# The experts' places in the gathered tensor, loaded as 448 rows each instead of by their own sizes

## The chip, the cores and the metric

One core of a Trainium2 chip. The metric is device time in microseconds of one execution, the median of three runs. The engines are TensorE (PE; its weight loads are listed as PEld), VectorE (DVE), ScalarE (ACT), GpSimd (POOL) and SyncE (SP). SP issues nearly all plain transfers, GpSimd the scattered ones.

## What is computed

Three stages on float32 data: a linear attention with decay, a mixture of 8 experts of which each token takes the best one, and a mixture of 4 experts of which each token takes all, weighted.

```
state = alpha[:, :, t, :, None] * state + k[:, :, t] (x) v[:, :, t];  y[:, :, t] = q[:, :, t] . state
x = y as (3072, 384)
logits = normed(x) @ normed(expert_emb).T / tau;  expert_idx = argmax(logits)
for e in range(8):                      # first mixture
    mask = expert_idx == e
    out[mask] = gate_w[mask, None] * (relu(x[mask] @ w1[e]) @ w2[e])
for e in range(4):                      # second mixture, x = out of the first
    out += p[:, e:e + 1] * (relu(x @ w1[e]) @ w2[e])
```

3072 tokens of 384 numbers; w1 is 384 x 1024 and w2 is 1024 x 384 for each expert.

## The kernel before

`attention_and_routing` computes the attention on all engines, chooses each token's expert and scatters the token's row (GpSimd, `scatter`) into the DRAM tensor `xs`, which has 3072 rows for each of the 8 experts. The first 448 rows of each expert were filled with zeros before (`prefill`). It also sorts the experts: place 0 is expert 0, places 1 to 7 are the others from the most chosen to the least. Where the text says "expert e" of the first mixture, it means the place e.

`experts` then runs the two mixtures. The list `WIN` (line 26) says how many tokens the fast path takes at each place: 448, 448, 432, 416, 404, 396, 392, 384; `W0` is the largest, 448. Place e goes through these steps:

- `window(e)` (lines 147 to 158) loads its rows from `xs` into a tile `xw` of 112 partitions, four rows (6144 bytes) to a partition. The transfer is issued by SP, line 154. For e above 0 the expert's number stands in a register of SP. The tile has two buffers.
- `xpose(e)` transposes the tile on PE (line 175) into PSUM; ScalarE copies it to `xh` (line 180), DVE puts the rest into `xl` (line 181), so that the product is made of three matmuls of reduced width.
- Eight units f follow, each with its own weights: `gemm1` (lines 120 to 122, 9 matmuls into `h`), `h_split` (ScalarE's `hh` in line 111, DVE's `hl` in line 112) and `g2` (lines 208 to 210, 9 matmuls from `hh` and `hl` into `o`). `g2` runs one unit behind `gemm1`.

The weights of one unit are 384 KB. `load_w` (line 57, SP) brings them into `wraw`, three buffers; `split_w` makes the two parts of `wu` from them, the first on ScalarE (line 67), the second on GpSimd (line 68), ten buffers. A new load waits until GpSimd has emptied a buffer. In unit (e, f) the program splits the unit nine places ahead, before it comes to the matmuls and to `h_split`.

Each engine takes its instructions in the order of the program. In unit f = 1 of place e it comes, for SP, to the weight load of that unit, then to `window(e + 2)`, then to the next weight loads. For ScalarE it comes to the split of a weight unit (line 67), then to `hh` of the current unit (line 111). In units 3 to 5 the three blocks of the next place are transposed.

The second mixture works on all 3072 tokens with the same units and loads nothing but weights.

Of the kernel before, what the change touches and what calls it, by code (L numbers as in the profile page):

```python
# [17 lines left out]
B, H, S, D = 4, 8, 768, 48  # L18
# [3 lines left out]
KD = DM // 128  # L22
NG = 8
CW = 129
# tokens that the fast path takes in: expert 0, then the others from the most chosen to the least
WIN = [448, 448, 432, 416, 404, 396, 392, 384]
W0 = max(WIN)
NR = 3072
# [3 lines left out]
@with_exitstack  # L32
def tile_main(ctx: ExitStack, tc: tile.TileContext, a: dict, out: bass.AP):
    nc = tc.nc

    const = ctx.enter_context(tc.tile_pool(name="const", bufs=1))
    small = ctx.enter_context(tc.tile_pool(name="small", bufs=2))
    dram = ctx.enter_context(tc.tile_pool(name="dram", bufs=1, space=bass.MemoryType.DRAM))

    xs = dram.tile([E1 * NR, DM], F32, name="xs")  # L40
    info_d = dram.tile([NT, 8], F32, name="info_d")

    # ---------------------------------------------------------------- weights
    units = [(0, e, f) for e in range(E1) for f in range(NFB)]
    units += [(1, e, f) for e in range(E2) for f in range(NFB)]
    wraw, wtile, ids = {}, {}, {}
    w_loaded, w_split = [0], [0]

    def load_w(n):
        while w_loaded[0] < min(n, len(units)):  # L50
            u = w_loaded[0]
            t = wst.tile([128, 2 * DM], F32, tag="wraw", name="wraw")
            src = a["wu"][u]
            if NFB <= u < E1 * NFB:
                e = a["wu"][0:E1 * NFB].rearrange("(e f) r c -> e f r c", f=NFB)
                src = e[bass.ds(ids[u // NFB], 1), u % NFB].rearrange("o r c -> (o r) c")
            nc.sync.dma_start(out=t, in_=src)
            wraw[u] = t
            w_loaded[0] += 1

    def split_w(n):
        while w_split[0] < min(n, len(units)):
            u = w_split[0]
            load_w(u + 1)
            r = wraw.pop(u)
            t = wun.tile([128, 2, 2 * DM], F32R, tag="wu", name="wu")
            nc.scalar.activation(out=t[:, 0], in_=r, func=AF.Copy)  # L67
            nc.gpsimd.tensor_tensor(out=t[:, 1], in0=r, in1=t[:, 0].bitcast(F32), op=ALU.subtract)  # L68
            wtile[u] = t
            w_split[0] += 1  # L70

    with tc.manual_schedule():
        ti = const.tile([128, 2, 128], F32, name="ti")
        ident = ti[:, 1]
        inf = const.tile([128, 24, 8], F32, name="inf")
        keep = {
            "ident": ident,
            "ti": ti,
            "ordi": const.tile([128, 8], I32, name="ordi"),
            "offi": const.tile([128, 8], I32, name="offi"),  # L80
            "posi": const.tile([128, 24], I32, name="posi"),
            "inf": inf,
            "flag": const.tile([1, 1], I32, name="flag"),
        }
        with ExitStack() as fast:
            wun = fast.enter_context(tc.tile_pool(name="wun", bufs=10))
            wst = fast.enter_context(tc.tile_pool(name="wst", bufs=3))
            scat = attention_and_routing(tc, a, small, keep, xs, info_d, wst, load_w, split_w)
            experts(fast, tc, a, keep, small, xs, info_d, scat, wtile, ids, load_w, split_w, out)

    bad = nc.values_load(keep["flag"][0:1, 0:1], min_val=0, max_val=1000)
    with tc.If(bad > 0):
        general(tc, a, ident, out)


def experts(ctx, tc, a, keep, small, xs, info_d, scat, wtile, ids, load_w, split_w, out):
# [24 lines left out]
            nc.tensor.matmul(ps, lhsT=w[:, 1, ks], rhs=xh(k), start=False, stop=False)  # L121
            nc.tensor.matmul(ps, lhsT=w[:, 0, ks], rhs=xl(k), start=False, stop=(k == KD - 1))  # L122

    # token info in the order of the experts
    infs = []

    def info(u):
# [11 lines left out]
    with ExitStack() as c1:  # L139
# [7 lines left out]
        def window(e):  # L147
            t = xwp.tile([W0 // 4, 4, DM], F32, tag="xw", name="xw")
            src = xs[0:W0, :]
            if e:  # L150
                src = xs.rearrange("(e r) d -> e r d", r=NR)[bass.ds(ids[e], 1), 0:WIN[e]].rearrange("o r d -> (o r) d")
            cs = [slice(k * 128, k * 128 + 128) for k in range(KD)] if e == 0 else [slice(0, DM)]
            for c in cs:
                ins = nc.sync.dma_start(
                    out=t[0:WIN[e] // 4, :, c], in_=src[:, c].rearrange("(p j) d -> p j d", j=4)
                )
                after(ins, scat, "all rows")
            xws[e] = t
# [146 lines left out]
def attention_and_routing(tc, a, small, keep, xs, info_d, wst, load_w, split_w):  # L305
# [5 lines left out]
    with ExitStack() as ctx:  # L311
# [18 lines left out]
        tau = c1.tile([128, 1], F32, name="tau")  # L330
# [6 lines left out]
        half = c1.tile([128, 6], F32, name="half")  # L337
# [29 lines left out]
        def c3(t, w):  # L367
            return t.rearrange("p (c w) -> p c w", w=w)

        # decay products of a chunk: after each step to its end (G), and their inverses (bf)  # L370
        def prep1(g, pp, c0=0, c1=3, part=2):
            al = tins[g, pp]
            lo, hi = 2 * CW * c0, 2 * CW * c1
# [178 lines left out]
        def route_b(r):  # L552
            u0, u1 = groups[r]
            n, sl = u1 - u0, slice(u0, u1)
            rt, mx, pr = state.pop(r)
            sv = small.tile([128, n, 8], F32, tag="sv", name="sv")
            si = small.tile([128, n], I32, tag="si", name="si", bufs=4)
            rank = [
                lambda: nc.vector.tensor_tensor(out=sv, in0=pr, in1=ohb[:, sl, :], op=ALU.mult),
                lambda: nc.vector.tensor_reduce(out=slotf[:, sl], in_=sv, op=ALU.add, axis=AX.X),  # L560
                lambda: nc.vector.tensor_scalar(
                    si, slotf[:, sl], float(E1 * NR - 1), 0.0, op0=ALU.min, op1=ALU.max
                ),
            ]
            g, root = root_v(nc, small, rt, ssq[:, sl], n, 128, "n")
            ex, exps = soft(nc, small, g, raw[:, sl, :], mx, n)
            # two chains of small steps, turn by turn
            chain = root + exps
            while rank or chain:
                for c in (rank, chain):  # L570
                    if c:
                        c.pop(0)()
            state[r] = si, ex
            if r < len(groups) - 1:
                count(r)
# [27 lines left out]
                tc.add_to_no_dep_group("xs", ins.ins)  # L603
                scat.append(ins)

        # ------------------------------------------------------------ start
        load_in(0, 0, 0, 259)
        nc.sync.dma_start(out=hmask, in_=a["hmask"])
        load_in(0, 0, 775, 1287)
# [166 lines left out]
        nc.vector.memset(ones, 1.0)  # L776
        nc.vector.memset(offc, 0.0)
        nc.vector.tensor_copy(cnt, pc)
        # the order of the experts: each one's number of experts before it, and each place's expert
        nc.vector.scalar_tensor_tensor(out=key, in0=cnt, scalar=8.0, in1=kadd, op0=ALU.mult, op1=ALU.add)  # L780
        nc.vector.tensor_tensor(out=gt3, in0=rows(key), in1=cols(key), op=ALU.is_gt)
        nc.vector.tensor_reduce(out=num, in_=gt3, op=ALU.add, axis=AX.X)
        nc.vector.tensor_tensor(out=sel, in0=rows(num), in1=cols(iot), op=ALU.is_equal)
        dot(srt, sel, iot)
        nc.vector.tensor_scalar(keep["ordi"], srt, float(E1 - 1), 0.0, op0=ALU.min, op1=ALU.max)
        # first columns of the places; as they are if no count is over its window, and else such that all is written
        dot(srt, sel, cnt)
        nc.vector.tensor_tensor(out=num, in0=srt, in1=wins, op=ALU.min)
        nc.vector.tensor_tensor_scan(offc[:, 1:8], ones[:, 1:8], num[:, 0:7], 0.0, op0=ALU.mult, op1=ALU.add)
        nc.vector.tensor_tensor(out=keep["offi"], in0=offc, in1=loff[:, 0, :], op=ALU.max)  # L790
        # places of the tokens in the order of the experts
        dot(off, gt3, cnt)
        nc.vector.tensor_tensor(out=off, in0=off, in1=loff[:, 1, :], op=ALU.subtract)
        pv = wk.tile([128, NU, 8], F32, tag="At", name="pv")
# [4 lines left out]
        nc.vector.tensor_reduce(out=pf, in_=pv, op=ALU.add, axis=AX.X)  # L799
        nc.vector.tensor_tensor(out=pf, in0=pf, in1=slotf, op=ALU.add)  # L800
        nc.vector.tensor_scalar(keep["posi"], pf, float(NT - 1), 0.0, op0=ALU.min, op1=ALU.max)
        # what the fast path doesn't cover
        fl = c1.tile([128, 3], F32, name="fl")
        ft = c1.tile([128, 3], F32, name="ft")
        nc.vector.memset(fl, 0.0)
# [17 lines left out]


def root_v(nc, pool, r, ss, n, parts, tag):
    """Twice the square root of ss from a first value r, to float32's accuracy: the tile and the steps."""
    g = pool.tile([parts, n], F32, tag=tag + "g", name="sq_g")
    return g, [
        lambda: nc.vector.tensor_scalar(g, r, 1e-18, None, op0=ALU.max),
# [10 lines left out]


def choose(nc, pool, wcon, raw, oh, n):
    """One-hot choice of the first largest of 8 (into oh), and the largest."""
    mx = pool.tile([128, n], F32, tag="mx", name="mx")
    nc.vector.tensor_reduce(out=mx, in_=raw, op=ALU.max, axis=AX.X)
    key = pool.tile([128, n, 8], F32, tag="key", name="key")
# [6 lines left out]


def soft(nc, pool, g2, raw, mx, n):
    """Exponentials of the logits less their largest, and the steps; g2 is twice the lengths of the rows."""
    rd = pool.tile([128, n], F32, tag="rd", name="rd")
    lg = pool.tile([128, n, 8], F32, tag="lg", name="lg")
    ex = pool.tile([128, n, 8], F32, tag="ex", name="ex")
# [15 lines left out]


def scale_rows(nc, pool, es_in, es, r, tau):
    """Rows of es_in over (their length + 1e-6) and tau, in place; es is their square sums."""
    g = run(root_v(nc, pool, r, es, 1, 8, "e"))
    nc.vector.tensor_scalar(g, g, 0.5, 1e-6, op0=ALU.mult, op1=ALU.add)  # L880
    nc.vector.tensor_scalar(g, g, tau[0:8, 0:1], None, op0=ALU.mult)
# [2 lines left out]


def general(tc, a, ident, out):
    """Any decay and any choice of experts: step by step over time, every expert over every token."""
    nc = tc.nc
    with ExitStack() as ctx:
        gc = ctx.enter_context(tc.tile_pool(name="gc", bufs=1))  # L890
# [153 lines left out]
def layout(inputs):  # L1044
# [2 lines left out]
    q, k, al = (np.asarray(inputs[n]) for n in ("q", "k", "alpha"))  # L1047

    def pairs(x):
        # -> (b, half, pp, row=(s d), chunk, pair in pp, 128)  # L1050
        x = x.reshape(B, 2, 2, 2, 2, 3, 128, D)  # b pp j s hf c i d
        return x.transpose(0, 4, 1, 3, 7, 5, 2, 6).reshape(NG, 2, 96, 3, 2, 128)

    aqk = np.zeros((NG, 2, 96, 775 + 1536), np.float32)
# [69 lines left out]
```

## Time and profile before

| | |
|---|---|
| median of 3 runs | 1264.83 us (1263.66 to 1265.12) |
| span of the profiled execution | 1262.2 us |
| its own time beside the span | not listed apart; the median is 2.6 us above the span |
| PE busy | 1192.4 us, 94% of the span |
| DVE, ACT, POOL busy | 426.1, 350.5, 320.9 us |
| mean granted TensorE clock | 0.972 |
| loads of `xw` | 10: three of 224.0 KB for place 0, and 672.0, 648.0, 624.0, 606.0, 594.0, 588.0, 576.0 KB for places 1 to 7 |

Times in rows are microseconds from the span's start. PE's matmuls are pipelined: a row's duration includes its filling, and the pace is read from the starts. A wait is put down to the instruction or the transfer that ended last before the waiting one began. "Granted clock" is the share of TensorE's full speed, 2.4 GHz.

### The profile page before, as it was taken

To read this page: it belongs to the slowest core of one execution; us is meant where nothing else is said; L and a number is where in the kernel's file an instruction comes from. 1 tells how busy PE (TensorE), PEld (TensorE's weight loads), DVE (VectorE), ACT (ScalarE), POOL (GpSimd) and SP (SyncE) were. 2 spreads that over 40 slices of the span, in tenths; PEclk is the share of its full clock that TensorE was granted. 3 is DMA by queue.
4 is the path that set the end of the run, shared out by engine and by line. 5 is a ranking of instruction groups with operands and counts; after the bars stand their busy time and mean duration, and the time that the engine had idled before them with its cause. 6 is when DMAs were issued, how large, how long until landed. Compare 5 with 4: busy or idle time off the path is not lost.

```text
span 1262.2 us, 16110 instructions
## 1 busy us (share of the span) xinstructions
PE 1192.4 (94%) x6565; PEld 1089.2 (86%) x6565; DVE 426.1 (34%) x791; ACT 350.5 (28%) x624; POOL 320.9 (25%) x223
## 2 busy tenths in 40 slices
PE   6987896987999999999999999999999999999996
PEld 4876785976999999999999999999999999999996
DVE  8998974221322222222222222212222222222221
ACT  3555553433544421111221111131111121111111
POOL 4565644544676620000130000040000021111111
PEclk9987897997999999999999999999999999999998
DMA  8845515423443420000020000020000010000000
GB/s 248 280 138 155 152 39 179 132 88 102 133 132 115 126 65 1 1 1 1 13 88 1 1 1 1 1 76 25 1 1 1 1 39 1 26 25 26 25 26 28
DMA packets 31260, 78.68 MB, mean 62 GB/s; under 512 B 7419, under 2 KB 12795, under 8 KB 29833
## 3 DMA queue, kind: packets, MB, share of 16 engines
q1 hardware_dynamic: 27337, 68.02, 17.7%
q0 software_dynamic: 3840, 9.54, 2.1%
q8 instruction: 53, 0.87, 0.3%
q14 instruction: 30, 0.25, 0.1%
HBM read 62.41 MB, written 15.14 MB: 61 GB/s over the span
## 4 chain that ended last, share of the span: by engine, by line
PE 81%; DVE 9%; DMA 4%; issue 3%; ACT 1%; POOL 1%; SPq 0%; ACTq 0%; POOLq 0%; DVEq 0%
PE h L120 13%; PE h L122 13%; PE h L121 13%; PE p L269 10%; PE p L268 10%; PE p L267 10%; PE o L208 3%; PE o L209 3%; PE o L210 3%; DMA wraw<-in_wu_dram 2%; DVE bf L393 2%; DVE G L380 2%; DVE At L443 1%; DMA v<-in_v_dram 1%; PE xt L175 1%
## 5 line engine op out<-in xcount | busy, mean ns | idle before, releaser
L112 DVE SCALAR_TENSOR_TENSOR hl<-h,hh 128x512 fp32r<-128x512 f32 (+8 forms) x264 | 171.9, 651 | 762.0 <-ACT hh L111 754.8
L68 POOL TENSOR_TENSOR wu<-wraw,wu 128x768 fp32r<-128x768 f32 x96 | 178.1, 1856 | 677.4 <-ACT wu L67 658.6
L111 ACT ACTIVATE hh<-h 128x512 fp32r<-128x512 f32 (+8 forms) x264 | 149.2, 565 | 670.4 <-PE h L122 668.7
L269 PE MATMUL p<-wu,hl 128*128 128x384 f32 x768 | 258.9, 337 | 0.0
L268 PE MATMUL p<-wu,hh 128*128 128x384 f32 x768 | 258.2, 336 | 0.0
L267 PE MATMUL p<-wu,hh 128*128 128x384 f32 x768 | 258.1, 336 | 0.0
L120 PE MATMUL h<-x,wu 128*128 128x512 f32 (+1 forms) x600 | 233.0, 388 | 0.0
L122 PE MATMUL h<-x,wu 128*128 128x512 f32 (+1 forms) x600 | 230.6, 384 | 0.0
L121 PE MATMUL h<-x,wu 128*128 128x512 f32 (+1 forms) x600 | 228.0, 380 | 0.0
L268 PEld LDWEIGHTS p<-wu,hh 128*128 128x128 f32 x768 | 144.3, 188 | 7.4
L267 PEld LDWEIGHTS p<-wu,hh 128*128 128x128 f32 x768 | 144.4, 188 | 7.1
L269 PEld LDWEIGHTS p<-wu,hl 128*128 128x128 f32 x768 | 144.3, 188 | 0.0
L122 PEld LDWEIGHTS h<-x,wu 128*128 128x128 f32 x600 | 112.6, 188 | 26.6
L121 PEld LDWEIGHTS h<-x,wu 128*128 128x128 f32 x600 | 112.8, 188 | 16.1
L120 PEld LDWEIGHTS h<-x,wu 128*128 128x128 f32 x600 | 112.8, 188 | 14.5
L67 ACT ACTIVATE wu<-wraw 128x768 fp32r<-128x768 f32 x96 | 80.8, 843 | 93.1 <-PE o L210 35.5
L208 PE MATMUL o<-hh,wu 128*128 128x448 f32 (+6 forms) x192 | 68.4, 356 | 14.5 <-ACT hh L111 14.5
L120 PE MATMUL h<-xh,wu 128*128 128x448 f32 (+6 forms) x192 | 70.4, 367 | 0.0
L280 POOL DMA_INDIRECT out_dram<-acc,toki x24 | 23.4, 974 | 183.4 <-DVE acc L276 178.5
L209 PE MATMUL o<-hl,wu 128*128 128x448 f32 (+6 forms) x192 | 68.4, 356 | 0.0
L438 PE MATMUL A<-qb,G 96*128 96x256 f32 x192 | 55.6, 435 | 13.6 <-ACT qb L415 8.3
L121 PE MATMUL h<-xh,wu 128*128 128x448 f32 (+6 forms) x192 | 68.4, 356 | 0.0
(150 smaller groups left out, 1172.9 us busy)
## 6 DMA issues: line engine op xcount, KB each, us to landing
wraw<-in_wu_dram SPq DMA_DIRECT2D x96, 384.0 KB, 3.0
tin<-in_aqk_dram SPq DMA_DIRECT2D x14, 866.6 KB
xs<-pre SPq DMA_DIRECT2D x8, 672.0 KB, 9.5
v<-in_v_dram SPq DMA_DIRECT2D x8, 576.0 KB, 5.3
tin<-in_aqk_dram SPq DMA_DIRECT2D x2, 384.0 KB, 6.8
xw<-xs SPq DMA_DIRECT2D x3, 224.0 KB
xw<-xs SPq DMA_DIRECT2D x1, 672.0 KB
xw<-xs SPq DMA_DIRECT2D x1, 648.0 KB
```

Of the source, the lines that this page charges most:

```text
L67: nc.scalar.activation(out=t[:, 0], in_=r, func=AF.Copy)
L68: nc.gpsimd.tensor_tensor(out=t[:, 1], in0=r, in1=t[:, 0].bitcast(F32), op=ALU.subtract)
L111: nc.scalar.activation(out=hh[:, 0:n], in_=ps, func=AF.Relu)
L112: nc.vector.scalar_tensor_tensor(out=hl[:, 0:n], in0=ps, scalar=0.0, in1=hh[:, 0:n].bitcast(F32), op0=ALU.max, op1=ALU.subtract)
L120: nc.tensor.matmul(ps, lhsT=w[:, 0, ks], rhs=xh(k), start=(k == 0), stop=False)
L121: nc.tensor.matmul(ps, lhsT=w[:, 1, ks], rhs=xh(k), start=False, stop=False)
L122: nc.tensor.matmul(ps, lhsT=w[:, 0, ks], rhs=xl(k), start=False, stop=(k == KD - 1))
L208: nc.tensor.matmul(o, lhsT=w[:, 0, ds], rhs=hh[:, 0:n], start=(f == 0), stop=False)
L209: nc.tensor.matmul(o, lhsT=w[:, 0, ds], rhs=hl[:, 0:n], start=False, stop=False)
L267: nc.tensor.matmul(o, lhsT=hh[:, js], rhs=w[:, 0, DM:2 * DM], start=(f == 0), stop=False)
L268: nc.tensor.matmul(o, lhsT=hh[:, js], rhs=w[:, 1, DM:2 * DM], start=False, stop=False)
L269: nc.tensor.matmul(o, lhsT=hl[:, js], rhs=w[:, 0, DM:2 * DM], start=False, stop=(f == NFB - 1))
```

## The change

The loads for places 1 to 7 take 448 rows of the expert, and the whole tile of 112 partitions, instead of `WIN[e]` rows and a quarter as many partitions. `xpose` still reads `WIN[e] // 4` partitions. Nothing else is changed; some comments are gone.

```
             src = xs[0:W0, :]
             if e:
-                src = xs.rearrange("(e r) d -> e r d", r=NR)[bass.ds(ids[e], 1), 0:WIN[e]].rearrange("o r d -> (o r) d")
+                src = xs.rearrange("(e r) d -> e r d", r=NR)[bass.ds(ids[e], 1), 0:W0].rearrange("o r d -> (o r) d")
             cs = [slice(k * 128, k * 128 + 128) for k in range(KD)] if e == 0 else [slice(0, DM)]
             for c in cs:
                 ins = nc.sync.dma_start(
-                    out=t[0:WIN[e] // 4, :, c], in_=src[:, c].rearrange("(p j) d -> p j d", j=4)
+                    out=t[:, :, c], in_=src[:, c].rearrange("(p j) d -> p j d", j=4)
                 )
```

The order of the instructions is the same on every engine. On SP's queue this is one of the six places that differ, the load for place 4 (line 154) between SP's register work (line 186) and the next weight load (line 57):

```order
 L186 ISA x2
 L154 ISA
-L154 DMA xw<-xs 101x1536
+L154 DMA xw<-xs 112x1536
 L57 ISA
 L57 DMA wraw<-in_wu_dram 128x768
```

No row moved; the transfer's shape went from 101 to 112 partitions of 1536 numbers. The places 2, 3, 5, 6 and 7 go from 108, 104, 99, 98 and 96 to 112 in the same way, and place 1 has 112 in both.

## Rows read from the trace of the kernel before

**Rows 1.** The page: span, and TensorE's busy time, share and instructions.

```profile
span 1262.2 us, 16110 instructions
...
PE 1192.4 (94%) x6565; PEld 1089.2 (86%) x6565; DVE 426.1 (34%) x791; ACT 350.5 (28%) x624; POOL 320.9 (25%) x223
```

**Rows 2.** Waits of PE, 203 to 1262 us: total, times, longest.

```profile
PE o L208 <- ACT hh L111: 14.5, 1, 14.5
```

**Rows 3.** By stretches: length, busy time (instructions) per engine, clock, DMA share, GB/s.

```profile
300.00:400.00 100.00, 100.00 (x557) 98.16 (x556) 29.12 (x51) 47.81 (x80) 66.33 (x43) 1.00 0.41 130
400.00:760.00 360.00, 360.00 (x1851) 330.66 (x1850) 85.30 (x138) 77.46 (x125) 50.04 (x29) 1.00 0.10 30
```

**Rows 4.** Timeline of PE: start, duration, line, operation, idle time before it.

```profile
276.82 0.36 PE L120 MATMUL h<-xh,wu 128*128 128x432 f32 x1
...
278.42 0.35 PE L122 MATMUL h<-xl,wu 128*128 128x432 f32 x1
293.26 0.73 PE L208 MATMUL o<-hh,wu 128*128 128x432 f32 x1 [14.49 <-ACT hh L111]
...
296.95 0.69 PE L175 MATMUL xt<-ti,xw 104*128 104x104 f32 x4
297.42 0.44 PE L120 MATMUL h<-xh,wu 128*128 128x432 f32 x1
...
301.38 0.44 PE L120 MATMUL h<-xh,wu 128*128 128x432 f32 x1
```

**Rows 5.** Timeline of ACT.

```profile
266.29 0.85 ACT L67 ACTIVATE wu<-wraw 128x768 fp32r<-128x768 f32 x1 [1.35 <-PE o L210]
...
270.31 0.84 ACT L67 ACTIVATE wu<-wraw 128x768 fp32r<-128x768 f32 x1
271.65 0.53 ACT L111 ACTIVATE hh<-h 128x432 fp32r<-128x432 f32 x1 [0.50 <-PE h L122]
291.95 0.84 ACT L67 ACTIVATE wu<-wraw 128x768 fp32r<-128x768 f32 x1 [19.77 <-DMA wraw<-in_wu_dram]
292.70 0.51 ACT L111 ACTIVATE hh<-h 128x432 fp32r<-128x432 f32 x1
```

**Rows 6.** The chain of work that ended last, in order of time: start, duration, what.

```profile
265.39 26.46 DMA wraw<-in_wu_dram
```

**Rows 7.** DMA issues: queue, operation, count, size, median time to landing.

```profile
wraw<-in_wu_dram SPq DMA_DIRECT2D x96, 384.0 KB, 3.0
...
xw<-xs SPq DMA_DIRECT2D x1, 606.0 KB
```

**Rows 8.** Timeline of SP's queue: start, duration, issue.

```profile
202.58 2.61 SPq L154 DMA_DIRECT2D xw<-xs  x2
...
263.38 0.29 SPq L154 DMA_DIRECT2D xw<-xs  x1
...
265.39 5.77 SPq L57 DMA_DIRECT2D wraw<-in_wu_dram  x1
```

**Rows 9.** Line 57 by itself: ns of one issue, min/median/max, first and last start.

```profile
L57 SPq DMA_DIRECT2D wraw<-in_wu_dram x96: 327/333/5772, 50.3 to 1034.4; - x96
```

**Rows 10.** By stretches, between the load for place 4 and PE's next matmul.

```profile
265.00:270.00 5.00, 5.00 (x26) 4.64 (x25) 1.98 (x4) 2.60 (x5) 3.20 (x3) 1.00 0.06 24
...
280.00:285.00 5.00, 0.00 (x0) 0.00 (x0) 0.00 (x0) 0.00 (x0) 0.00 (x0) 0.86 0.06 26
285.00:290.00 5.00, 0.00 (x0) 0.00 (x0) 0.00 (x0) 0.00 (x0) 0.00 (x0) 0.50 0.07 27
```

**Rows 11.** By stretches, at the loads of 104, 99, 98 and 96 partitions.

```profile
232.00:236.00 4.00, 4.00 (x21) 3.65 (x20) 0.63 (x1) 1.70 (x3) 1.85 (x1) 1.00 0.80 222
...
310.00:314.00 4.00, 4.00 (x22) 3.82 (x21) 0.61 (x1) 1.46 (x3) 3.08 (x3) 1.00 0.76 247
339.00:343.00 4.00, 4.00 (x23) 3.92 (x22) 0.59 (x1) 1.36 (x2) 3.26 (x3) 1.00 0.83 268
367.00:371.00 4.00, 4.00 (x24) 4.00 (x23) 0.58 (x1) 1.48 (x3) 3.28 (x3) 1.00 0.89 259
```

**Rows 12.** The DMA queues from 206 to 232 us, GB/s in 40 equal slices.

```profile
GB/s 271 180 255 345 317 241 222 227 189 147 57 24 0 255 321 28 38 189 345 85 274 251 123 232 255 24 0 24 246 326 9 0 0 25 184 340 66 14 0 0
```

**Rows 13.** Waits of ACT, 195 to 470 us.

```profile
ACT wu L67 <- DMA wraw<-in_wu_dram: 22.6, 4, 19.8
```

More of the change, by code (lines that the diff above doesn't have):

```diff
@@ L150, in window @@
             if e:
-                src = xs.rearrange("(e r) d -> e r d", r=NR)[bass.ds(ids[e], 1), 0:WIN[e]].rearrange("o r d -> (o r) d")
+                src = xs.rearrange("(e r) d -> e r d", r=NR)[bass.ds(ids[e], 1), 0:W0].rearrange("o r d -> (o r) d")
             cs = [slice(k * 128, k * 128 + 128) for k in range(KD)] if e == 0 else [slice(0, DM)]
@@ L154, in window @@
                 ins = nc.sync.dma_start(
-                    out=t[0:WIN[e] // 4, :, c], in_=src[:, c].rearrange("(p j) d -> p j d", j=4)
+                    out=t[:, :, c], in_=src[:, c].rearrange("(p j) d -> p j d", j=4)
                 )
```

## The prediction

> **What bounds the kernel now.** I read first where TensorE is idle, since it is busy for 1192.4 us of 1262.2 [rows 1]. The list of its waits from 203 us to the end has a single entry: 14.5 us, once, in L208 for ScalarE's hh [rows 2]. The table by stretches agrees: PE is busy 100.00 of 100 and 360.00 of 360 us after it, at full clock [rows 3]. So behind 203 us this kernel is TensorE work end to end with one hole, and a change to the loads of the expert part can gain only in that hole, or lose by making new ones.
>
> Second, what the hole is. PE's last matmul before it starts at 278.42, the next one at 293.26 [rows 4]. ScalarE's order of work tells why: after the hh of 271.65 it should split the next weight unit (L67), and that waits 19.77 us for a load of wraw. The hh that PE wants (292.70) stands behind it on the same engine [rows 5]. That up to ten split units lie ready doesn't help, because it is ScalarE's queue that is blocked, not the supply of split weights.
>
> Third, which load that is. The chain of waits runs through a wraw load issued at 265.39, which takes 26.46 us [rows 6], where such a load takes 3.0 in the median of 96 [rows 7]. On SP's queue the instruction ahead of it is the load of expert 4's place (263.38), and SP needs 5.77 us to issue the weight load behind it [rows 8], against a median of 0.333 [rows 9]. While nothing but this is in flight, the DMA engines are busy by 0.06 to 0.07 of the sixteen and move 24 to 27 GB/s [rows 10]: that is one engine out of sixteen. Expert 4's load is 404 rows, 101 partitions, 101 x 6144 B = 620,544 B (606.0 KB in [rows 7]); at 25 GB/s this is 24.8 us. From about 264.4 us it would end near 289, and the part of the weight loads that lies behind it on that engine accounts for the rest up to 291.85. The sum closes: one engine carries the whole 101-partition load, the weight load waits for its turn there, ScalarE for the weight load, PE for ScalarE.
>
> The other loads of this line do nothing of the kind. Those of 104, 99, 98 and 96 partitions stand in stretches with 0.76 to 0.89 of all engines busy at 222 to 268 GB/s, and PE is busy 4.00 of 4 us in each [rows 11].
>
> **Why one engine.** The rows show that 101 partitions went through one engine and that 104, 99, 98 and 96 went through many; they do not show the rule. The nearest row to the new load is expert 1's, which has today the very form that all get: 112 partitions, 672 KB, a source chosen by a register. It was issued from 202.58 on, together with the next one [rows 8], and at 213.8 us (the thirteenth of 40 slices of 0.65 us from 206 on) nothing is moved at all [rows 12]; on one engine at 25 GB/s its 688,128 B would need 27.5 us, to 230. So the form with 112 is wide. The Trainium skill, "DMA: Bandwidth & Descriptors", section "Why a DMA increments its semaphore by 16 and not by 1", has the rule: a DMA uses the largest count up to 16 that divides the slowest dimensions, by which 108, 104, 101, 99, 98 and 96 partitions get 12, 13, 1, 11, 14 and 16 engines and 112 gets 16. The trace agrees for 101 (0.06 of sixteen) and doesn't separate the others; by that rule the sum below is the same as by the rows.
>
> **The change, part by part.**
> 1. *The 101-partition load becomes a 112-partition one.* It removes the hole. Its cost is read between like points on PE. L120 of one unit starts at 276.82; the next unit begins, after 18 matmuls and 4 transposes, at 297.42. The same step takes 301.38 - 297.42 = 3.96 us one unit later at full clock [rows 4]. So the unit should have started at 280.78, and 297.42 - 280.78 = **16.64 us** is lost. Of these, 293.26 - 278.62 = 14.64 are the hole (278.42 plus one matmul step; eight steps from 276.82 on take 1.60, so one is 0.20), and 2.0 the clock: in the hole the granted clock fell from 1.00 to 0.50, that is from 2.4 to 1.2 GHz [rows 3, 10], and the nine matmuls after it take 296.95 - 293.26 = 3.69 us for 1.80 [rows 4]. Nothing of this lies beside other work of PE, and all of PE's later work follows directly, so all of it comes off the end.
> 2. *What comes in its place at that point.* 688,128 B over many engines. At the 222 to 268 GB/s of [rows 11] that is 2.6 to 3.1 us, and with the 393,216 B of the weight load behind it 4.0 to 4.9 us after 263.38, so the unit is there at about 268. ScalarE wants it at about 273.9: its last split began at 270.31 [rows 5], and a unit is 18 matmul steps, 3.6 us. The slack of some 6 us covers it; without that slack the cost would be 1:1 on ScalarE, then on PE. Price 0.
> 3. *The five other loads* (108, 104, 99, 98, 96) grow to 112. With the 101 one, 16 + 32 + 44 + 52 + 56 + 64 = 264 rows of 1536 B, 405,504 B, 1.6 us of transfers at 259 GB/s (the row at 367 us) in total, 0.1 to 0.4 us each, each with PE full beside it ([rows 11]; for the 108 one, at 205 us, by the list of PE's waits [rows 2]) and the same slack of some 6 us before the weight unit behind it is wanted. Lower bound of the price: 0. Upper bound: all of it, 1.6 us. I take 0.
> 4. *Everything else.* PE, DVE, ScalarE and GpSimd keep their instructions in the same order and shape, and the transposes still read only the expert's own partitions; the rows added to the tile are read by nobody. SP waits for the same semaphores. Price 0.
>
> **Sum.** The profiled execution: 1262.2 - 16.6 = 1245.6 us of span. The median of the runs is 2.6 us above this span, which I carry over unchanged: 1264.83 - 16.64 = **1248.2 us**.
>
> After the hole the next thing to be late would be ScalarE's splits. Apart from the long one, the three other waits of L67 for a weight load are together 22.6 - 19.8 = 2.8 us [rows 13], and PE waited in none of them.
>
> **The rivals.**
> - *The hole shrinks but doesn't go.* ScalarE could still stand in L67 for some us, because SP's queue holds the window and the weights in one row. For it: a single blocked split stops PE one unit later. Against: at the 96-partition load, as wide as the new one by its 0.89, PE has no gap [rows 11]. Halfway between 0 and 14.6 us, with the clock's 2.0 still paid: 9.3 us left, 1257.5.
> - *101 was not the cause* but something the new load shares with the old (where expert 4's rows lie, a collision with the stores of GpSimd). Then it takes 67,584 B more through one engine, 2.7 us, and the end is at 1267.5, which is at the edge of what can be told from no change (0.2%, 2.5 us). Against: the loads before and after it come from the same tensor beside the same stores, without a hole [rows 11]; the partition count is what sets it apart.
> - *Slower: the new loads are narrow.* If a 112-partition load whose source a register picks ran on one engine, each of six would make such a hole: 16.6 + 2.7 = 19.3 us each, 116 in all, less the 16.6 of now: 1364. It decides from three engines down: 688,128 B at 25 GB/s each take 9.2 us on three and 6.9 on four, against some 8 us from the window's issue until its followers are late (the slack of 6 and the 2 between the two issues). Against it stands expert 1's load, gone within 12 us with no wait on PE. The same page gives about 27 GiB/s for an engine, section "Specifications"; with it this rival's loads would take 23.7 us each for 27.5, and its end would be some 23 us lower. The rows show 24 to 27 GB/s, so the trace doesn't bear that figure out.
>
> **How the numbers follow.** Hole gone: 0.92. Part of it left: 0.03. Another cause: 0.03. Narrow loads: 0.02. The prediction is the first one's time. Its own bounds: at best the 2.8 us of ScalarE's other waits for weights turn into time too, 1245.4; at worst a short wait remains that still lets the clock fall and costs the 2.0 us, 1250.2, and half the spread of the three runs (1263.66 to 1265.12) is 0.7, so 1250.9. The other three cases hold 0.08 and may stay outside: range 1245.4 to 1250.9. Faster takes the first two cases, 0.95; the third is split between no change (0.02) and slower (0.01), and with the fourth slower is 0.03.
>
> **What would show it.** In the profile after: no wait of L208 for hh in the list of PE's waits behind 203 us; ScalarE's longest wait of L67 for wraw under 3 us; no stretch near 265 to 292 us with one engine's worth of transfers (0.06, 25 GB/s); a granted clock of 1.00 in every stretch from 210 to 1000 us; seven loads of 672 KB by a register in place of one, and no issue of a weight load over 1 us behind them; a span near 1245.6. A hole that stays at the same place would refute the partition count; six holes, one per expert, the width of 112; and a span some us over 1245.6 without a hole would say that the added bytes cost what I put at 0.

## The result, and the profile after

The median of four runs is 1247.94 us (1246.82 to 1249.04) against 1264.94 (1263.66 to 1265.12) of the kernel before, 17.0 us less; the ratio is 0.9866 with a 95% interval of 0.9852 to 0.988. The prediction was 1248.2.

The page of the kernel after, its span and first table, which answer to [rows 1]:

```profile
span 1247.3 us, 16110 instructions
...
PE 1189.9 (95%) x6565; PEld 1088.5 (87%) x6565; DVE 424.8 (34%) x791; ACT 351.3 (28%) x624; POOL 321.2 (26%) x223
```

The span is only 14.9 us shorter than in the profile of before. That is not the expert part: the profiled execution was the slowest of its four (1249.04), and its front, the attention, ended later. The timeline of SP's queue gives the point at which the first load of `xw` is issued, in the kernel after:

```profile
200.90 1.97 SPq L154 DMA_DIRECT2D xw<-xs  x3
```

and in the kernel before:

```profile
198.70 1.97 SPq L154 DMA_DIRECT2D xw<-xs  x3
```

From there to the end it is 1247.3 - 200.90 = 1046.4 us after and 1262.2 - 198.70 = 1063.5 before, a difference of 17.1 us. I call this stretch the expert part and use it below for every run, since the front is the same code in all of them and yet begins its first load anywhere between 196.0 and 202.0 us.

The waits of PE from 200 us on, of the kernel after (columns as in [rows 2]):

```profile
PE pfl L814 <- DVE ft L812: 5.9, 1, 5.9
PE xt L175 <- DMA xw<-xs: 0.9, 1, 0.9
```

Both lie ahead of the first transposes at 204 us and are in the kernel before too. The wait of L208 for hh is gone. By stretches, in the columns of [rows 3]:

```profile
210.00:300.00 90.00, 90.00 (x463) 83.18 (x463) 23.99 (x39) 41.12 (x65) 53.33 (x33) 1.00 0.49 142
300.00:400.00 100.00, 100.00 (x565) 98.85 (x564) 29.90 (x52) 48.87 (x81) 66.41 (x44) 1.00 0.45 129
400.00:745.00 345.00, 345.00 (x1763) 315.73 (x1762) 80.83 (x130) 70.29 (x113) 40.49 (x23) 1.00 0.09 26
```

In these stretches, and from 745 to 985 us as well, PE is busy throughout at a granted clock of 1.00. The unit that needed 297.42 - 276.82 = 20.60 us in [rows 4] is, on PE's timeline after:

```profile
278.63 0.36 PE L120 MATMUL h<-xh,wu 128*128 128x432 f32 x1
...
282.51 0.44 PE L120 MATMUL h<-xh,wu 128*128 128x432 f32 x1
```

282.51 - 278.63 = 3.88 us, so 16.72 us came off at this one place. The remaining 0.4 of the 17.1 lies ahead of it: from the first load to this unit it is 276.82 - 198.70 = 78.12 us before and 278.63 - 200.90 = 77.73 after, because the granted clock rose some 1.0 us earlier behind the first transposes in this execution. From the unit behind it to the end it is 964.8 us in both (1262.2 - 297.42 and 1247.3 - 282.51).

What stood behind the hole is now ordinary. ScalarE's waits, 195 to 470 us, and the issues of line 57 (columns of [rows 13] and [rows 9]):

```profile
ACT wu L67 <- DMA wraw<-in_wu_dram: 3.1, 3, 2.1
```

```profile
L57 SPq DMA_DIRECT2D wraw<-in_wu_dram x96: 327/333/863, 50.4 to 1019.5; - x96
```

The longest wait for a weight load fell from 19.8 to 2.1 us and the longest issue from 5.77 to 0.86 us.

### The profile page after: what moved, and what is told of

It is laid out like the page before. It is cut to its first block, busy times and chain, and to the rows that moved or that the text cites. A ratio compares the mean times of both kernels' runs of the same rounds, so it can differ in the third digit from the quotient of the medians.

```text
span 1247.3 us, 16110 instructions
## 1 busy us (share of the span) xinstructions
PE 1189.9 (95%) x6565; PEld 1088.5 (87%) x6565; DVE 424.8 (34%) x791; ACT 351.3 (28%) x624; POOL 321.2 (26%) x223
## 4 chain that ended last, share of the span: by engine, by line
PE 84%; DVE 7%; issue 4%; DMA 1%; POOL 1%; SPq 0%; ACT 0%; POOLq 0%; ACTq 0%
PE h L120 13%; PE h L122 13%; PE h L121 13%; PE p L269 10%; PE p L268 10%; PE p L267 10%; PE o L208 3%; PE o L209 3%; PE o L210 3%; DVE bf L393 1%; PE A L438 1%; DVE G L380 1%; DVE At L443 1%; PE fin L513 1%; PE xt L175 1%
## 5 line engine op out<-in xcount | busy, mean ns | idle before, releaser
L120 PEld LDWEIGHTS h<-x,wu 128*128 128x128 f32 x600 | 112.8, 188 | 14.5
L122 PE MATMUL h<-xl,wu 128*128 128x448 f32 (+6 forms) x192 | 68.0, 354 | 0.0
L208 PE MATMUL o<-hh,wu 128*128 128x448 f32 (+6 forms) x192 | 67.7, 352 | 0.0
```

Source lines behind the costliest of these rows:

```text
L120: nc.tensor.matmul(ps, lhsT=w[:, 0, ks], rhs=xh(k), start=(k == 0), stop=False)
L208: nc.tensor.matmul(o, lhsT=w[:, 0, ds], rhs=hh[:, 0:n], start=(f == 0), stop=False)
```

## The experiments

The theory: one DMA engine carried all 101 partitions, because of that number; the weight load waited behind it, ScalarE for the weight load, PE for ScalarE. Each experiment is an edit of the kernel before. All touch only the load of place 4, but for two: the one on 109 partitions, which touches six loads, and the last, which changes ScalarE's order in every unit and no load. Line numbers move by a few in them.

**Place 4 alone.**

```
+            n = 112 if e == 4 else WIN[e] // 4
...
-                    out=t[0:WIN[e] // 4, :, c], in_=src[:, c].rearrange("(p j) d -> p j d", j=4)
+                    out=t[0:n, :, c], in_=src[:, c].rearrange("(p j) d -> p j d", j=4)
```

(the source is cut to 4 * n rows in the same way).

> The load of place 4 alone is widened from 101 to 112 partitions; the five others keep 108, 104, 99, 98 and 96. Theory (the 101-partition load goes through one DMA engine and is the only one that costs): all of the gain, 1248 us within 1 us, no hole on PE near 280 us. Rival (the other five loads also cost something that the change takes away): between 1250 and 1262 us. Rival (where place 4's rows lie makes it slow): 1265 to 1268 us, the hole stays.

Measured: 1248.2 us (1247.4 to 1249.79), ratio 0.9872 (0.9855 to 0.9888). The expert part is 1245.6 - 199.81 = 1045.8 us, 0.6 less than with all six widened, and behind 205 us PE waits for nothing. So one of the six widened loads gives the whole gain; the five others give nothing, and their added bytes cost nothing that shows. It also rules out the place: the same expert's rows, eleven partitions more of them, and no hole.

**The same rows in two loads.**

```
+                n = WIN[e] // 4
+                for lo, hi in [(0, 96), (96, n)] if e == 4 else [(0, n)]:
...
+                        out=t[lo:hi, :, c], in_=src[4 * lo:4 * hi, c].rearrange("(p j) d -> p j d", j=4)
```

> The same 101 partitions of place 4, no row more, in two transfers of 96 and 5 partitions. Theory (it is the count of partitions of one transfer, not the bytes, the rows or their place): 1248 us within 1 us, no hole. Rival (something about these rows or this place): 1265 us, the hole stays.

Measured: 1247.9 us (1247.21 to 1249.19), ratio 0.9866 (0.9849 to 0.9882); expert part 1246.5 - 199.98 = 1046.5 us. Not one row more is loaded than before, and the hole is gone. The bytes and the rows were never the matter; the shape of the transfer was.

**103 and 102 partitions.** The edit of the first experiment with 103, and with 102, for 112.

> Place 4's load has 103 partitions, the next prime number. By the rule of the largest divisor up to 16: one engine, 632,832 B at 25 GB/s are 25.3 us, a hole on PE of about 15.1 us and 2 for the clock, some 0.5 us over the kernel before: 1265.4 us. Rival (101 was a case of its own): 1248 us.

> Place 4's load has 102 partitions, between the two primes. By the rule of the largest divisor up to 16: six engines, 626,688 B at 6 x 25 GB/s are 4.2 us, no hole, 1248 us. Rival (counts that are no multiple of 4 or 8, or merely near 101, are slow): a hole of over 10 us, 1260 to 1266 us.

Measured, one run each: 1262.12 us for 103 and 1244.38 for 102. The fronts differ (first load at 198.98 and 196.00 us); the expert parts are 1260.3 - 198.98 = 1061.3 and 1242.6 - 196.00 = 1046.6 us, that is 14.9 and 0.2 over the kernel after. With 103 partitions PE has its hole again, in its list of waits from 255 to 330 us,

```profile
PE o L209 <- ACT hh L111: 13.8, 1, 13.8
```

and the stretches show one engine at work:

```profile
280.00:285.00 5.00, 0.00 (x0) 0.00 (x0) 0.00 (x0) 0.00 (x0) 0.00 (x0) 0.64 0.07 27
285.00:290.00 5.00, 0.00 (x0) 0.00 (x0) 0.00 (x0) 0.00 (x0) 0.00 (x0) 0.50 0.06 25
```

With 102, between two primes, there is no such wait. Its load shows in the rates of the DMA queues from 260 to 270 us (40 slices of 0.25 us):

```profile
GB/s 61 246 332 381 332 160 147 111 74 49 74 98 147 147 147 172 147 184 233 307 283 319 233 199 185 128 51 74 111 246 258 272 360 382 234 172 131 61 25 0
```

The slices at 147 are 6 x 24.5, and 6 is the largest divisor of 102 that is not above 16; being near 101 does no harm. The hole at 103 is 0.7 us shorter than the 14.5 at 101 where 0.5 longer was expected; a single run doesn't settle a difference of that size.

**106 and 111 partitions: two engines, three engines.** The same edit.

> Place 4's load has 106 partitions, by the rule of the largest divisor two engines: 651,264 B at 50 GB/s are 13.0 us. In the kernel before 24.8 us of transfer make a hole of 14.6, so 13.0 make one of 2.8 us, with up to 2 for the clock: 1251 to 1253 us. Rival (only a single engine costs): 1248 us.

> Place 4's load has 111 partitions, by the rule three engines: 681,984 B at 75 GB/s are 9.1 us. By the same subtraction (24.8 us of transfer, 14.6 us of hole, so 10.2 us are free) there is no hole: 1248 us. The prediction's own threshold, about 8 us free and so a small hole at three engines, would give 1249 to 1251 us.

Measured: 106 gives 1253.42 us (1252.95 to 1253.79), ratio 0.991 (0.9887 to 0.9934); 111 gives 1248.47 (1247.92 to 1251.08), ratio 0.9871 (0.9848 to 0.9894). Expert parts 1053.0 and 1047.3 us, 6.6 and 0.9 over the kernel after. The stretches show the engines being counted. For 106, after the weight loads' other parts have gone:

```profile
277.00:279.00 2.00, 1.08 (x6) 0.69 (x4) 0.00 (x0) 0.00 (x0) 0.00 (x0) 1.00 0.12 51
```

0.12 of sixteen, 51 GB/s: two engines. For 111:

```profile
279.00:280.40 1.40, 1.40 (x9) 1.33 (x8) 0.00 (x0) 0.00 (x0) 0.00 (x0) 1.00 0.19 70
```

0.19, 70 GB/s: three. PE's waits for `hh` and `hl` from 200 us on, 106 first:

```profile
PE o L209 <- ACT hh L111: 3.9, 1, 3.9
```

```profile
PE o L210 <- DVE hl L112: 0.3, 2, 0.2
PE o L209 <- ACT hh L111: 0.2, 1, 0.2
```

With three engines ScalarE still waits 5.49 us for the weight load, on its timeline,

```profile
280.61 0.84 ACT L67 ACTIVATE wu<-wraw 128x768 fp32r<-128x768 f32 x1 [5.49 <-DMA wraw<-in_wu_dram]
```

and PE stops there for only 0.4 in all (0.2 for `hh`, 0.2 for `hl`): when ScalarE blocks, PE has the rest of a unit to do. So what is free is ScalarE's slack and this rest together, and the point from which a narrow load costs lies between three engines and two. The expectation for 106 was 1251 to 1253; the hole is 3.9 us where 2.8 was worked out, and the clock cost more too. Its share is read between like points on PE, as in the prediction (106 partitions):

```profile
276.13 0.36 PE L120 MATMUL h<-xh,wu 128*128 128x432 f32 x1
...
277.73 0.35 PE L122 MATMUL h<-xl,wu 128*128 128x432 f32 x1
281.99 0.73 PE L209 MATMUL o<-hh,wu 128*128 128x432 f32 x1 [3.91 <-ACT hh L111]
...
286.27 0.71 PE L120 MATMUL h<-xh,wu 128*128 128x432 f32 x1
...
291.23 0.44 PE L120 MATMUL h<-xh,wu 128*128 128x432 f32 x1
```

The two units take 10.14 and 4.96 us where one takes 3.96 at full clock [rows 4], so 7.2 us are lost; 281.99 - 277.93 = 4.1 of them are the hole and 3.1 the clock, against 2.0 behind the long hole. (The expert part shows 6.6 in place of 7.2; two executions without a hole differ by as much as that, 0.6.) A stretch behind PE's restart, 106 partitions:

```profile
285.00:290.00 5.00, 5.00 (x21) 4.60 (x20) 0.69 (x2) 1.78 (x3) 3.03 (x3) 0.65 0.43 139
```

A hole of 3.9 us took the granted clock down just as one of 14.5 did; its mean of 0.65 here comes of one part of the stretch at 0.50, which is 1.2 GHz, and the rest at 1.00.

**All six loads on one engine.**

```
+            n = 109 if e > 1 else 112
```

> The loads of places 2 to 7 have 109 partitions each, a prime number. Theory: one engine each, 669,696 B at 25 GB/s are 26.8 us, a hole of 16.6 us and 2 for the clock behind each of six loads: 112 us over the changed kernel, 1360 us, six holes. Rival (place 4 is special): one hole at most, 1248 to 1267 us.

Measured, one run: 1370.24 us, where 1360 was expected; expert part 1368.4 - 201.39 = 1167.0, which is 120.6 over the kernel after. PE's list of waits, whole expert part:

```profile
PE o L209 <- ACT hh L111: 106.1, 6, 22.1
```

Six holes, 17.7 us in the mean, and (120.6 - 106.1) / 6 = 2.4 each for the clock. The first is the longest, 22.1; the five others run from 15.4 to 18.2, about the 16.6 expected. Why the first is longer wasn't followed. Every place pays, so place 4 was special by its number alone. This is the slower rival of the prediction, put on the chip.

**The load on ScalarE's queue.**

```
-                src = xs.rearrange("(e r) d -> e r d", r=NR)[bass.ds(ids[e], 1), 0:WIN[e]].rearrange("o r d -> (o r) d")
+                src = xs.rearrange("(e r) d -> e r d", r=NR)[bass.ds(ids["w"] if e == 4 else ids[e], 1), 0:WIN[e]].rearrange("o r d -> (o r) d")
...
-                ins = nc.sync.dma_start(
+                eng = nc.scalar if e == 4 else nc.sync
+                ins = eng.dma_start(
...
+            if e == 4:
+                ids["w"] = nc.scalar.value_load(keep["ordi"][0:1, e:e + 1], min_val=0, max_val=E1 - 1)
```

> Place 4's load keeps its 101 partitions but is issued by ScalarE on its own queue instead of by SP, at the same place of the program. Theory in the strict form (the weight load waits because its part stands behind the window's parts in one queue of one engine): the load still takes some 25 us or more on one engine, but the weight loads pass it, at about half that engine's rate, and PE has no hole: 1248 to 1250 us. Rival (the engine itself is taken, whatever queue it comes from): the hole stays, 1263 to 1266 us.

Measured: 1255.28 us (1252.74 to 1256.29), ratio 0.992 (0.9894 to 0.9945); expert part 1052.6 us, 6.2 over the kernel after. Neither range was met, and the trace tells in part why. The chain of waits:

```profile
273.25 35.55 DMA xw<-xs
308.93 3.20 DMA wraw<-in_wu_dram
```

The load with 101 partitions takes 35.55 us here, from 273.25 to 308.80. While it runs, the weight loads on SP's queue pass it; seven of them land 7.5 us after their issue in the median, in place of 3.0. PE's stretch from there to 295 us:

```profile
273.30:295.00 21.70, 21.70 (x117) 20.50 (x116) 5.79 (x10) 9.09 (x15) 14.02 (x9) 1.00 0.39 121
```

PE is full where it had its hole: sharing the engine is not enough to stop it, standing behind the load in SP's queue was. The lost time comes later and in another way. SP's waits, 255 to 335 us:

```profile
SPq L57 <- DMA xw<-xs: 12.6, 1, 12.6
```

A weight load in the next place isn't issued until the 101-partition load has landed, ScalarE then waits 7.8 us for it and PE 2.9:

```profile
PE o L211 <- ACT hh L111: 2.9, 1, 2.9
```

The granted clock falls to 0.50 in this hole too, which makes up the rest of the 6.2. Why SP waits for that landing there the profile doesn't say, and it wasn't tried further. So the step "the part stands behind it in one queue" is borne out for the first hole; as a remedy another queue is worse than a good partition count.

**hh ahead of the split.**

```
                 if e or f > 1:
-                    split_w(e * NFB + f + 9)
+                    load_w(e * NFB + f + 9)
...
                 hs[e, f] = h_split(ps, n)
+                if e or f > 1:
+                    split_w(e * NFB + f + 9)
```

> The kernel before with its 101-partition load, but in each unit ScalarE makes hh of the current unit ahead of the split of the unit nine places on; the loads are issued in the old order. Theory (PE stops because the hh that it wants stands behind the blocked split on ScalarE): the blocked split now lets one more hh out, so PE runs one unit of 3.6 us longer and the hole shrinks from 14.5 to about 11 us, total about 1261 us. Rival (PE stops for the weights themselves or for the transposed rows): the hole keeps its 14.5 us, 1265 us.

Measured: 1262.0 us (1260.42 to 1262.94), against 1265.63 of the kernel before, run beside it; ratio 0.9971 (0.996 to 0.9981). The medians are 3.6 us apart, one unit. ScalarE's timeline:

```profile
273.87 0.53 ACT L111 ACTIVATE hh<-h 128x432 fp32r<-128x432 f32 x1 [2.32 <-PE h L122]
292.25 0.84 ACT L67 ACTIVATE wu<-wraw 128x768 fp32r<-128x768 f32 x1 [17.86 <-DMA wraw<-in_wu_dram]
```

One hh more gets out before the split blocks, and PE's wait goes from 14.5 to 12.2 us (some 11 was expected):

```profile
PE o L208 <- ACT hh L111: 12.2, 1, 12.2
```

The expert part is 1258.6 - 198.58 = 1060.0 us, 3.5 less than before. The weight load lands no earlier, so it is the order on ScalarE that turns its delay into a hole on PE.

## Why the prediction was right

- *Where the time lay.* One hole, 16.64 us with its clock. Measured at that place: 16.72; in the medians 17.0. Right. The 0.4 us that the two profiled executions differ by ahead of this place is not of the change, and that the median lies within 0.3 us of the forecast is in part luck. The span is 1247.3 and not the 1245.6 forecast, because the first load came 2.2 us later in this execution.
- *One engine, by the partition count.* At first this rested on 0.06 of sixteen and a rule of the Trainium skill, "DMA: Bandwidth & Descriptors", section "Why a DMA increments its semaphore by 16 and not by 1". The runs show it: one engine at 103 and in 109's six holes, two at 106 (0.12), three at 111 (0.19), six at 102 (147 GB/s), and there is no hole at 112, or at 96 and 5. The traces agree with the rule at each count whose engines the rows tell: 101, 102, 103, 106, 109 and 111.
- *The five other loads and the added bytes at 0.* Widening place 4 alone gives 1248.2 against 1247.94 us, and neither profile has a wait on PE behind 205 us. Right.
- *ScalarE's order.* Shown by hh ahead of the split: 3.6 us, a unit.
- *The weight load behind the window in one queue.* Shown for the hole by the load on ScalarE's queue, where PE ran through it.
- *The slower rival.* Its price was 116 us for 112 partitions on one engine in six places; with 109 it was 120.6. Its threshold, "from three engines down", was off by one: three engines cost 0.4 us of PE's waits at this place (0.9 us of expert part, little more than the 0.6 by which executions without a hole differ), two cost 6.6. What was left out is that PE goes on for the rest of its unit when ScalarE blocks. This term decided nothing in the sum.
- *The 27 GiB/s for an engine* of the Trainium skill, "DMA: Bandwidth & Descriptors", section "Specifications": this is 29 GB/s, and the runs stay below it, as the rows of before did, with 24 to 27 GB/s for one engine, 51 for two and 70 for three.

## What to carry to other kernels

Look at the partition count of every transfer, not only at its bytes: of two loads that differ by one partition in a hundred, one took six engines and the other one. If the count follows from data sizes, round it up to a number with a large divisor up to 16 (112 is 7 x 16) and read rows that nobody uses, or cut the load in two; both cost nothing here. When TensorE stops, follow the wait back from queue to queue: the narrow load did no harm to its own reader, the transposes of place 4 that begin 63 us after its issue, but to the weight load queued behind it, and through that to ScalarE and then to TensorE.

## What the runs showed of the hardware

- A narrow transfer holds up the issuing queue as well: SP's issue of the weight load behind the 101-partition load took 5.77 us [rows 8] and up to 9.63 us with 109 partitions. It took at most 0.86 us in the kernel after, 0.76 with 106 and 0.85 with 111 partitions (two and three engines), and 0.94 where the 101 partitions came from ScalarE's queue.
- A hole of 3.9 us on PE cost more by the clock (3.1 us, between like points, one execution) than one of 14.5 (2.0 us): a short stop is not cheap in proportion.
- The front of this kernel, the same code in every run, reaches the first load of `xw` anywhere between 196.0 and 202.0 us. A single run's whole time can be off by several us in either direction. The stretch from a fixed event to the end is steadier: 1045.8 to 1046.6 us in the four executions without a hole (the kernel after, place 4 alone, two loads, 102 partitions).
